# One weight prepared per pair of half steps, transfers issued in pairs, and two small results in one accumulator bank

## The chip, the cores and the metric

The kernel runs on one core of a Trainium2 chip. The metric is the device time of one execution in microseconds (us). The core's engines work at the same time and wait for each other through semaphores: PE (TensorE, matrix products and transposes; its results go to eight accumulator banks in PSUM), DVE (VectorE), ACT (ScalarE), POOL (GpSimd) and SP, which here only issues transfers.

## The reference

Three layers follow each other, all in float32. The first is an attention with two parts: a coarse one over keys and values averaged in groups of four, and a local one in which a query sees the seven keys around it. The second is a mixture of eight experts, whose weights per token come from eight rounds of row and column normalising. The third is a gated product `(x w_a * x w_b) w_out`.

```python
q_d = q.reshape(B, H, Sd, 4, D).mean(axis=3)        # k_d, v_d alike; B, H, S, D = 2, 8, 576, 64
out_up = np.repeat(sm_attn(q_d, k_d, v_d), 4, axis=2)
mask = np.abs(pos[:, None] - pos[None, :]) < 4
out_local = np.matmul(softmax(np.where(mask, scores, -1e9)), v)
x = out_up + out_local                              # (1152, 512) after a transpose
logits = x @ w_gate                                 # P: exp, then 8 times rows and columns normalised
for e in range(8):
    out += P[:, e:e+1] * (np.maximum(x @ w1[e], 0) @ w2[e])
return (out @ w_a) * (out @ w_b) @ w_out
```

## The kernel before, in words

Every float32 factor is kept as a high and a low part (`xh`, `xl`; a weight block's `hi`, `lo`), and each product takes three matmuls. A weight block is made from a raw tile: ACT casts it (line 138), and DVE or POOL subtracts (line 139). All of this is `split`. Raw tiles are two halves of 256 KB times two; two of them can be staged at once, and a new one is fetched when an old one has been used up.

Attention has 24 items, each a pair of heads times a third of a sequence. They run in a software pipeline, the generator `side()`: in step s, item s is transposed and scored, and items s-1 to s-4 are in later stages. A step has two halves, separated by `yield`. The main program runs the first layer of the first two weight units (half of expert 0 each) meanwhile, and calls `side_step()` for a half step at a time. The order of all instructions on each engine is fixed when the program is built.

The stages that matter here, with the lines of the profile:

- `a1` (lines 991, 1005) transposes an item's queries and, where a new pair of heads begins, its keys, which takes a second bank. `a2` and `a4` copy and scale them on ACT; DVE sums the keys in fours (line 1049).
- `b1` and `b1c` score (line 61); `b2` takes maxima on DVE; `b3` exponentiates on ACT (lines 1100 and 1103); `b4` normalises: `pdn` on DVE (line 1120), `p` on POOL (line 1117).
- `c1` transposes the coarse weights `pdn` (line 1130, two instructions into `pt2`) and the local weights `p` (line 1135, three instructions into `pt`); `c2` copies the coarse ones (line 1141, DVE or ACT), `c3` the local ones on ACT (line 1149).
- `d1` multiplies both with v (line 61) into one bank `ps`: columns 0 to 191 local, 192 to 239 coarse. `d2a` scales the coarse part on ACT (`od`, line 1170), `d2` adds both on DVE (`x`, line 1176), and `d3` splits the sum into `xh` (ACT, line 1186) and `xl` (POOL, line 1187).

In the second half of step s the order of the calls is `d1(s-3)`, `d2a(s-3)`, `b3(s-1)`, `c1(s-2)`, `d2(s-3)`, `c2(s-2)`. Items 0 to 10 are scored (`b1`, `b1c`) in the first half of the step after their own; from item 11 on in the second half of their own step, and there `b1c(s)`, four matmuls with `kd`, stands between `d1` and `c1` (steps 11 to 23). So `c1` of item i (1 to 23) always follows `d1` of item i-1 in the same half step.

All attention results use tiles named `at` from a ring of six banks (`psa`). A tile that is asked for gets the bank of the tile six requests ago and waits until that is read. A step takes a bank in `a1` (two with keys), one in `b1`, two in `c1`, one in `d1`.

Around it, `step()` prepares weight blocks by the numbers in `share`, one number for each call, and advances attention by three half steps in two calls. `load_some()` issues one transfer of a raw tile per half step, from a list `coming`.

Of the kernel before, what the change touches and what calls it, by code (L numbers as in the profile page):

```python
# [8 lines left out]
F32 = mybir.dt.float32  # L9
# [11 lines left out]
def attn_moe_glu_kernel(  # L21
# [16 lines left out]
    nc = tc.nc  # L38
# [21 lines left out]
    def mm(o, l, r, start, stop, check=True):  # L60
        nc.tensor.matmul(out=o, lhsT=l, rhs=r, start=start, stop=stop, skip_group_check=not check)  # L61
# [34 lines left out]
    def dve(us, after=None):  # L96
        M.dve = max(M.dve, M.pe if after is None else after) + us

    def act(us):
        M.act = max(M.act, M.pe) + us  # L100
# [20 lines left out]
    def new_block(uses):  # L121
        i = nring[0] % NSLOT
        assert RING[i] is None or RING[i].uses == 0
        nring[0] += 1
        t = wr.tile([128, 1024], F32R, tag=f"w{i}", name=f"w{i}")
        RING[i] = Block(t[:, 0:512], t[:, 512:1024], uses)
        return RING[i]

    def pool(us):
        M.pool = max(M.pool, M.pe) + us  # L130
# [3 lines left out]
    def split(b, raw, k=1, low=None):  # L134
        hi, lo = b.hi, b.lo
        if k > 1:
            hi, lo = (t.rearrange("p (k f) -> p k f", k=k) for t in (hi, lo))
        nc.scalar.copy(out=hi, in_=raw)  # L138
        lows.append(lambda: (low or nc.vector).tensor_tensor(  # L139
            out=lo, in0=raw, in1=hi.bitcast(F32), op=ALU.subtract  # L140
        ))
        if not put_off[0]:
            lows.pop()()
        act(0.6)
        if low is None:
            dve(0.75, 0.0)
        else:
            pool(1.35)
# [10 lines left out]
    wq = []  # L159
# [57 lines left out]
    hold, nsteps, freed, coming = [True], [0], [0], []  # L217

    def fetch():
        while lq and staged[0] < 2:  # L220
            r = lq.pop(0)
            staged[0] += 1
            r.place = stg.tile([128, 2, 512], F32, tag="raw", name="raw", bufs=2)
            r.dmas = r.load(r.place)
            coming.append(r)
            r.at = M.pe
            if not hold[0]:
                r.tile

    def load_some():  # L230

        if nsteps[0] >= max(6, freed[0] + 2):
            fetch()
        while coming and not coming[0].dmas:
            coming.pop(0)
        if coming and nsteps[0] not in NO_LOAD:
            coming[0].dmas.pop(0)()

    def halves(load, left):

        rs = [Raw(lambda t, j=j: load(t, j), left[j]) for j in range(len(left))]
        lq.extend(rs)
        return rs

    def queue_plain(u, uses=6, low=None):

        u.w = {}
        rs = halves(u.load1, (2, 2))
        for i in range(2):
            for j in range(2):  # L250
                def piece(i=i, j=j):
                    b = u.w[i, j] = new_block(uses)
                    split(b, rs[j].tile[:, :, 256 * i:256 * i + 256], 2, low)
                    rs[j].used()
                wq.append(Task(piece, 0.0 if low else 0.68, 1.35 if low else 0.0, ready=rs[j].ready, slot=True))

    def queue_combined(u, low=None):

# [71 lines left out]
    for i, w in enumerate((w_a, w_b, w_out)):  # L330
        t = dram.tile(list(w.shape), F32, name=f"w32_{i}")
        w32.append(t)
        src = w.bitcast(I32).rearrange("a b -> (a b)").rearrange("(c p f) -> c p f", p=128, f=2 * CH)
# [64 lines left out]
    def loader(src):  # L398
        return lambda t, j: [
            lambda k=k: nc.sync.dma_start(out=t[:, k], in_=src[:, 2 * j + k]) for k in range(2)  # L400
        ]

    def half_loader(src):
# [11 lines left out]

        return load

    units = []
    for e in range(E):
        for hf in range(2):  # L420
            u = Unit()
            u.e, u.hf = e, hf
            load = loader if units else half_loader
            u.load1 = load(w1[e][:, hf * 512:(hf + 1) * 512].rearrange("(k p) f -> p k f", p=128))
            u.load2 = loader(w2[e][hf * 512:(hf + 1) * 512, :].rearrange("(k p) f -> p k f", p=128))
            units.append(u)
# [3 lines left out]
    for g in range(GU):  # L430
        u = Unit()
# [447 lines left out]
    ready = [-1]  # L879
    attn_stack = ExitStack()  # L880
    ap_ = attn_stack.enter_context(tc.tile_pool(name="ap", bufs=1, side="right"))
    at = attn_stack.enter_context(tc.tile_pool(name="at", bufs=3, side="right"))
    psa = attn_stack.enter_context(tc.tile_pool(name="psa", bufs=6, space=PSUM))
# [97 lines left out]
        )  # L981
        v_d[b, hp] = vd

    pA, pB, pC, pD = {}, {}, {}, {}

    def a1(i, b, u, hp):

# [136 lines left out]

    def c1(i, b, u, hp):
        p, pd = pB.pop(i)
        pt = psa.tile([128, 512], F32, tag="at", name="at")
        pt2 = psa.tile([128, 512], F32, tag="at", name="at")
        for kh in range(2):
            nc.tensor.transpose(  # L1130
                pt2[0:72, kh * 128:kh * 128 + R],
                pd.rearrange("p (t k) -> p k t", k=2)[:, kh], ident[:R, :R],
            )
        for c in range(NC):
            nc.tensor.transpose(pt[0:W, c * 128:(c + 1) * 128], p[:, c], ident)  # L1135
        pC[i] = pt, pt2
# [15 lines left out]
    def d1(i, b, u, hp):  # L1152
        a, d = pC.pop(i)
        hs = slice(2 * hp, 2 * hp + 2)
        ps = psa.tile([128, 512], F32, tag="at", name="at")
        n = NC * 16
        pd_ = ps[:, UT:UT + n]
        for kh in range(2):
            for h in range(2):
                mm(pd_[64 * h:64 * h + 64], v_d[b, hp][:, kh, h], d[:, kh, h], kh == 0, kh == 1)  # L1160
        for c in range(NC):
            for h in range(2):
                ph = slice(64 * h, 64 * h + 64)
                mm(ps[ph, c * 64:(c + 1) * 64], v_win[b, u, hp][:, c, h], a[:, c, ph], True, True)
        pD[i] = ps, pd_
# [92 lines left out]
    order = [(0, u, hp) for hp in range(HP) for u in range(2)]  # L1258
# [9 lines left out]
    def side():  # L1268
# [17 lines left out]
        for s in range(n + 5):  # L1286
# [34 lines left out]
            if s >= TURN:  # L1321
                do(b1, s)
            do(d1, s - 3)
            if s >= TURN:
                do(b1c, s)
            do(d2a, s - 3)
            do(b3, s - 1)
            do(c1, s - 2)
            do(d2, s - 3)
            do(c2, s - 2)  # L1330
# [8 lines left out]
    TURN = 11  # L1339
# [33 lines left out]
    with tc.manual_schedule():  # L1373
# [19 lines left out]
        for h in range(2):  # L1393
            ph = slice(64 * h, 64 * h + 64)
            for base, cm, st_ in ((9, 1, -1), (-3, -1, 1)):
                nc.gpsimd.affine_select(
                    out=mw[ph], in_=mw[ph], compare_op=ALU.is_ge, fill=-1e30, base=base,
# [8 lines left out]


        for u, low in zip(units[:2], (nc.gpsimd, None)):
            queue_plain(u, low=low)
        for u in units[:2]:  # L1410
            queue_out(u)
        queue_combined(units[2], nc.gpsimd)
# [58 lines left out]
        def side_step():  # L1471
            if not closed:
                nsteps[0] += 1
                load_some()
            if gens[0] is None:
                return
            try:
                next(gens[0])
            except StopIteration:
                if closed:  # L1480
                    gens[0] = None
                else:
                    close_attention()
# [3 lines left out]
        tmp_stack = ExitStack()  # L1487
        turn = 0.0
        nside = 0
        share = [0, 0, 1, 1, 1, 1, 2, 2, 1, 2, 1]  # L1490

        def step():
            nonlocal turn
# [71 lines left out]
        for x, names in (("gh0", ("t1", "b12")), ("gl0", ("b22", "b21"))):  # L1565
            t = gp.tile([128, 1536], F32, tag=x, name=f"t{x}")
# [4 lines left out]
        for x, G in (("h", GH), ("l", GL)):  # L1571
            t = [g0p.tile([128, 1024], F32R, tag=f"g{x}_0{n}", name=f"g{x}_0{n}") for n in range(2)]
# [29 lines left out]
        for x, G in (("h", GH), ("l", GL)):  # L1602
            o = 16 if x == "l" else 0
            t = [gp.tile([128, 1296], F32R, tag=f"g{x}{n}", name=f"g{x}_1{n}") for n in range(2)]
# [93 lines left out]
```

## Time and profile before

| | us |
|---|---|
| median of 3 runs (lowest 1048.74) | 1049.03 |
| profiled execution, whole | 1048.58 |
| span from its first to its last instruction | 1046.8 |
| PE busy | 1037.9 (99%) |
| DVE, ACT, POOL busy | 656.1, 481.1, 528.3 |

Attention, with work of expert 0 beside it, fills about the first 140 us. The rest of the span is experts and the gated product, which the diff does not touch. In the rows, times start at the first instruction; "idle before" is the time in which the engine had nothing before the instruction, with what ended it. PE's ends are modelled, its starts are recorded.

### The profile page before, as it was taken

How to read it: one execution, taken by the hardware profiler on the slowest of the kernel's cores; microseconds unless marked ns; L12 is line 12 of the kernel's file. 1: busy time of each engine (PE TensorE's matmuls, PEld its weight loads, DVE VectorE, ACT ScalarE, POOL GpSimd, SP SyncE). 2: the span in 40 equal slices, each digit the busy share in tenths (PEclk: the TensorE clock that was granted, in tenths of full speed). 3: DMA queues.
4: the chain of work that ended last, by engine and by line, in shares of the span. 5: the costliest groups of instructions: out<-in, count | busy, mean ns of one | idle time of the engine just before them, and what ended most of it. 6: DMA issues, size and time to landing. Idle time of an engine off the chain costs nothing.

```text
span 1046.8 us, 18525 instructions
## 1 busy us (share of the span) xinstructions
PE 1037.9 (99%) x6940; PEld 937.7 (90%) x6940; DVE 656.1 (63%) x1328; ACT 481.1 (46%) x1173; POOL 528.3 (50%) x531
## 2 busy tenths in 40 slices
PE   8999999999999999999999999999999999999998
PEld 6888889899899998999899899989999899999997
DVE  7785548666566565656656565656444685767664
ACT  6764424555444444445444454544343744332320
POOL 5633136647464555647364564746444544655521
PEclk9999999999999999999999999999999999999999
DMA  9662001243323323242433323232110101221102
GB/s 194 149 165 62 10 1 41 71 132 94 117 80 115 102 71 106 66 129 83 112 104 88 106 67 113 95 113 82 61 61 21 41 21 61 61 61 41 34 8 90
DMA packets 80728, 84.53 MB, mean 81 GB/s; under 512 B 35328, under 2 KB 54784, under 8 KB 80640
## 3 DMA queue, kind: packets, MB, share of 16 engines
q1 hardware_dynamic: 78864, 82.92, 27.4%
q8 instruction: 54, 0.88, 0.3%
q10 hardware_dynamic: 1776, 0.44, 0.2%
q14 instruction: 34, 0.28, 0.1%
HBM read 71.54 MB, written 11.80 MB: 80 GB/s over the span
## 4 chain that ended last, share of the span: by engine, by line
PE 95%; DVE 2%; POOL 1%; ACT 1%; issue 1%; DMA 0%; DVEq 0%; ACTq 0%; POOLq 0%
PE g L61 90%; PE at L61 3%; PE at L1130 1%; PE at L1135 1%; PE g L855 0%; PE at L991 0%; POOL w L139 0%; PE at L1005 0%; DVE G L696 0%; ACT p L1100 0%; DMA raw<-w 0%; POOL gl L692 0%; DVE kd L1049 0%; DVE b L621 0%; DVE rsum L1112 0%
## 5 line engine op out<-in xcount | busy, mean ns | idle before, releaser
L61 PE MATMUL g<-w,gh 128*128 128x512 f32 x1314 | 408.0, 392 | 0.0
L61 PE MATMUL g<-xh,w 128*128 128x256 f32 (+2 forms) x1472 | 316.0, 300 | 0.0
L692 POOL TENSOR_TENSOR gl<-G,gh 128x256 fp32r<-128x256 f32 (+1 forms) x216 | 177.8, 832 | 250.1 <-ACT gh L690 244.0
L61 PEld LDWEIGHTS g<-w,gh 128*128 128x128 f32 x1314 | 239.6, 188 | 43.6
L61 PE MATMUL g<-w,gl 128*128 128x512 f32 x657 | 257.6, 392 | 0.0
L61 PEld LDWEIGHTS g<-xh,w 128*128 128x128 f32 x1472 | 242.8, 188 | 2.4
L61 PE MATMUL g<-xl,w 128*128 128x256 f32 (+2 forms) x736 | 220.0, 299 | 0.0
L696 DVE TENSOR_TENSOR G<-g,G 128x256 f32<-128x256 f32 (+1 forms) x400 | 168.3, 451 | 68.6 <-PE g L61 34.5
L61 PE MATMUL g<-Th,w 128*128 128x256 f32 (+1 forms) x960 | 207.5, 294 | 0.4 <-DVE G L696 0.3
L139 DVE TENSOR_TENSOR w<-raw,w 128x512 fp32r<-128x512 f32 x129 | 116.2, 910 | 79.4 <-ACT w L138 79.3
L61 PEld LDWEIGHTS g<-Th,w 128*128 128x128 f32 x960 | 159.7, 188 | 3.3 <-issue 1.0
L548 DVE SCALAR_TENSOR_TENSOR acc<-g,P,acc 128x512 f32<-128x512 f32 x126 | 94.2, 748 | 94.9 <-PE g L61 91.6
L61 PEld LDWEIGHTS g<-w,gl 128*128 128x128 f32 x657 | 123.4, 188 | 26.3
L61 PE MATMUL g<-Tl,w 128*128 128x256 f32 (+1 forms) x480 | 140.7, 293 | 0.0
L61 PEld LDWEIGHTS g<-xl,w 128*128 128x128 f32 x736 | 138.2, 188 | 2.6 <-issue 0.2
L690 ACT CAST gh<-G 128x256 fp32r<-128x256 f32 (+1 forms) x216 | 93.6, 433 | 100.7 <-DVE G L706 85.7
L138 ACT CAST w<-raw 128x512 fp32r<-128x512 f32 x181 | 109.6, 620 | 63.4 <-POOL raw L269 48.3
L688 ACT ACTIVATE G<-G 128x256 f32<-128x256 f32 (+1 forms) x168 | 74.2, 442 | 103.1 <-DVE G L696 103.1
L139 POOL TENSOR_TENSOR w<-raw,w 128x512 fp32r<-128x512 f32 x52 | 68.5, 1324 | 57.7 <-ACT w L138 57.7
L61 PEld LDWEIGHTS g<-Tl,w 128*128 128x128 f32 x480 | 90.3, 188 | 2.1
L381 POOL TENSOR_TENSOR dec<-dec 128x384 int32<-128x384 int32 x48 | 49.4, 1029 | 77.7 <-ACT dec L357 52.3
L139 POOL TENSOR_TENSOR w<-s,w 128x512 fp32r<-128x512 f32 x40 | 55.6, 1391 | 21.1 <-ACT w L138 21.0
(179 smaller groups left out, 990.9 us busy)
## 6 DMA issues: line engine op xcount, KB each, us to landing
raw<-in_moe_w_dram SPq DMA_DIRECT2D x128, 256.0 KB
w<-dec SPq DMA_DIRECT2D x48, 192.0 KB
dec<-in_moe_w_a_dram SPq DMA_DIRECT2D x16, 384.0 KB
dec<-in_moe_w_b_dram SPq DMA_DIRECT2D x16, 384.0 KB
dec<-in_moe_w_out_dram SPq DMA_DIRECT2D x16, 384.0 KB
raw<-w SPq DMA_DIRECT2D x48, 128.0 KB
raw<-w SPq DMA_DIRECT2D x12, 256.0 KB
out_dram<-acc SPq DMA_DIRECT2D x9, 256.0 KB
```

The source lines that it names most:

```text
L61: nc.tensor.matmul(out=o, lhsT=l, rhs=r, start=start, stop=stop, skip_group_check=not check)
L138: nc.scalar.copy(out=hi, in_=raw)
L139: lows.append(lambda: (low or nc.vector).tensor_tensor(out=lo, in0=raw, in1=hi.bitcast(F32), op=ALU.subtract))
L381: nc.gpsimd.tensor_tensor(out=t, in0=t, in1=raw[:, :, 0], op=ALU.add)
L548: nc.vector.scalar_tensor_tensor(out=a, in0=ps, scalar=P[:, tt, u.e:u.e + 1], in1=a, op0=ALU.mult, op1=ALU.add)
L688: nc.scalar.activation(out=src, in_=src, func=AF.Relu)
L690: nc.scalar.copy(out=h, in_=src)
L692: nc.gpsimd.tensor_tensor(out=l, in0=src, in1=h.bitcast(F32), op=ALU.subtract)
L696: nc.vector.tensor_tensor(out=o, in0=bank_, in1=b, op=ALU.add)
L1130: nc.tensor.transpose(pt2[0:72, kh * 128:kh * 128 + R], pd.rearrange("p (t k) -> p k t", k=2)[:, kh], ident[:R, :R],)
L1135: nc.tensor.transpose(pt[0:W, c * 128:(c + 1) * 128], p[:, c], ident)
```

## The change

The diff has four parts.

1. **Shared bank.** `d1` of item i leaves its bank in `shared`, and `c1` of item i+1 puts the two coarse transposes in columns 256 to 511 of that bank rather than in a bank of its own.
2. **Column halves.** The second unit's first-layer weights are loaded in halves by columns (all four row blocks, 256 columns) rather than by rows. `queue_plain` then uses up the first half after two blocks, not three.
3. **Transfers in pairs.** After half step 23, `load_some` issues both transfers of a raw tile together.
4. **Shares.** `share` becomes 0, 0, 1, 1, 3, 1, 1, 1, 2, 1, 1.

```diff
         if coming and nsteps[0] not in NO_LOAD:
-            coming[0].dmas.pop(0)()
+            for _ in range(2 if nsteps[0] > 2 * TURN + 1 else 1):
+                if coming[0].dmas:
+                    coming[0].dmas.pop(0)()
...
-    def queue_plain(u, uses=6, low=None):
+    def queue_plain(u, uses=6, low=None, columns=False):
...
-                    split(b, rs[j].tile[:, :, 256 * i:256 * i + 256], 2, low)
-                    rs[j].used()
-                wq.append(Task(piece, 0.0 if low else 0.68, 1.35 if low else 0.0, ready=rs[j].ready, slot=True))
+                    if columns:
+                        r = rs[i]
+                        raw = r.tile[:, j].rearrange("p (k f) -> p k f", k=2)
+                    else:
+                        r = rs[j]
+                        raw = r.tile[:, :, 256 * i:256 * i + 256]
+                    split(b, raw, 2, low)
+                    r.used()
+                r = rs[i if columns else j]
+                wq.append(Task(piece, 0.0 if low else 0.68, 1.35 if low else 0.0, ready=r.ready, slot=True))
...
+    def column_loader(src):
+        def load(t, i):
+            d = t.rearrange("p a (b c) -> p (a b) c", b=2)
+            return [
+                lambda k=k: nc.sync.dma_start(
+                    out=d[:, 2 * k:2 * k + 2], in_=src[:, 2 * k:2 * k + 2, 256 * i:256 * i + 256]
+                ) for k in range(2)
+            ]
+
+        return load
...
-            load = loader if units else half_loader
+            load = (half_loader, column_loader)[len(units)] if len(units) < 2 else loader
...
     def c1(i, b, u, hp):
         p, pd = pB.pop(i)
+        pt2 = shared.pop(i, None)
+        if pt2 is None:
+            pt2 = psa.tile([128, 512], F32, tag="at", name="at")
+        pt2 = pt2[:, 256:512]
         pt = psa.tile([128, 512], F32, tag="at", name="at")
-        pt2 = psa.tile([128, 512], F32, tag="at", name="at")
...
         ps = psa.tile([128, 512], F32, tag="at", name="at")
+        if i + 1 < len(order):
+            shared[i + 1] = ps
...
-            queue_plain(u, low=low)
+            queue_plain(u, low=low, columns=u is units[1])
...
-        share = [0, 0, 1, 1, 1, 1, 2, 2, 1, 2, 1]
+        share = [0, 0, 1, 1, 3, 1, 1, 1, 2, 1, 1]
```

PE and POOL keep their instructions in the same order; what PE waits for moves. This is PE in the second half of step 12 before (`at` with its number is the bank's tile: 1143 is `d1`'s, 1163 is `pt2`, 1162 is `pt`):

```order
L61 MATMUL at_1143<-pdT_1069,vd1_397 64x48 x3
L61 MATMUL at_1143<-plT_1092,vw_782 64x64 [waits DMAHW6_49]
L61 MATMUL at_1143<-plT_1092,vw_782 64x64
L61 MATMUL at_1134<-kd1_1112,qT0_112 64x144 [waits DVE_49,Activation_49]
L61 MATMUL at_1134<-kd1_1112,qT0_112 48x144
L1130 MATMUL at_1163<-ident_76,pdn_1100 72x112 [waits PE_49]
L1130 MATMUL at_1163<-ident_76,pdn_1100 72x112
L1135 MATMUL at_1162<-ident_76,p0_114 70x128 [waits PE_49,Pool_49]
```

The same place in the changed kernel, where lines 1130 and 1135 have become 1153 and 1158:

```order
L61 MATMUL at_1134<-pdT_1060,vd1_396 64x48 x3
L61 MATMUL at_1134<-plT_1083,vw_776 64x64 [waits DMAHW6_49]
L61 MATMUL at_1134<-plT_1083,vw_776 64x64
L61 MATMUL at_1125<-kd1_1103,qT0_112 64x144 [waits DVE_49,Activation_49]
L61 MATMUL at_1125<-kd1_1103,qT0_112 48x144
L1153 MATMUL at_1134<-ident_76,pdn_1091 72x112 [waits Activation_49]
L1153 MATMUL at_1134<-ident_76,pdn_1091 72x112
L1158 MATMUL at_1153<-ident_76,p0_114 70x128 [waits PE_49,Pool_49]
```

The first coarse transpose now writes `at_1134`, the bank into which `d1` has just put its products, and waits for ACT: the semaphore's value is reached by the `od` of that same bank. It is so in all 23 items from 1 on. On DVE, `x` (`at_1134,od_1147`), which waited for ACT alone, now waits for PE's second coarse transpose as well.

On ACT the casts change places against `od`, the copy of the coarse products. This is ACT in step 13 before, between the relu's output `gh` and `od`:

```order
L1186 CAST xh_79<-x_1169 128x192
L500 ACTIVATE gh1_97<-g1_1206 128x384
L138 CAST w6_1221<-raw_817 128x512
L500 ACTIVATE gh1_97<-g1_1224 128x384
L138 CAST w7_1239<-raw_909 128x512
L1170 ACTIVATE od_1264<-at_1251 128x48
```

And there in the changed kernel:

```order
L1211 CAST xh_79<-x_1159 128x192
L520 ACTIVATE gh1_97<-g1_1199 128x384
L138 CAST w6_1214<-raw_902 128x512
L138 CAST w7_1217<-raw_902 128x512
L138 CAST w8_1220<-raw_1166 128x512
L520 ACTIVATE gh1_97<-g1_1223 128x384
L138 CAST w9_1238<-raw_1166 128x512
L1195 ACTIVATE od_1263<-at_1250 128x48
```

Two more casts stand here, ahead of the second relu; in each of the two steps that follow, one cast stands ahead of `od` rather than two.

## Rows read from the trace of the kernel before

**Rows 1.** The page's parts 1 and 2: PE's busy time, PE's granted clock.

```profile
PE 1037.9 (99%) x6940; PEld 937.7 (90%) x6940; DVE 656.1 (63%) x1328; ACT 481.1 (46%) x1173; POOL 528.3 (50%) x531
...
PEclk9999999999999999999999999999999999999999
```

**Rows 2.** The page's part 4: the chain of waits, by engine.

```profile
PE 95%; DVE 2%; POOL 1%; ACT 1%; issue 1%; DMA 0%; DVEq 0%; ACTq 0%; POOLq 0%
```

**Rows 3.** Busy us by stretch: PE, PEld, DVE, ACT, POOL; granted clock, DMA share, GB/s.

```profile
0.00:10.00 10.00, 8.17 (x76) 5.75 (x76) 4.87 (x33) 4.58 (x13) 2.22 (x14) 1.00 0.84 164
...
20.00:30.00 10.00, 9.86 (x153) 8.28 (x154) 8.19 (x30) 8.53 (x34) 8.90 (x13) 1.00 0.94 194
...
60.00:70.00 10.00, 9.09 (x115) 7.87 (x111) 8.63 (x23) 8.64 (x29) 3.66 (x5) 1.00 0.76 208
```

**Rows 4.** What PE waited for in 0 to 200: us, times, longest.

```profile
PE at L1005 <- ACT pd L1103: 0.9, 1, 0.9
PE at L1130 <- DVE pdn L1120: 0.6, 2, 0.4
```

**Rows 5.** Timeline of PE, steps 11 and 23: start, us, instructions.

```profile
44.15 0.53 PE L61 MATMUL at<-plT,vw 70*64 70x64 f32 x12
44.52 0.41 PE L61 MATMUL at<-kd,qT 128*64 128x144 f32 x4
44.86 0.41 PE L1130 MATMUL at<-ident,pdn 112*72 112x112 f32 x2
...
116.15 0.42 PE L1130 MATMUL at<-ident,pdn 112*72 112x112 f32 x2
```

**Rows 6.** Timeline of ACT at the same two places.

```profile
44.79 0.21 ACT L1170 ACTIVATE od<-at 128x48 f32<-128x48 f32 x1 [0.52 <-PE at L61]
...
116.08 0.21 ACT L1170 ACTIVATE od<-at 128x48 f32<-128x48 f32 x1 [0.74 <-PE at L61]
```

**Rows 7.** Timeline of PE: coarse transposes of items 4, 6 and 8.

```profile
23.03 0.42 PE L1130 MATMUL at<-ident,pdn 112*72 112x112 f32 x2
...
29.41 0.42 PE L1130 MATMUL at<-ident,pdn 112*72 112x112 f32 x2
...
35.74 0.42 PE L1130 MATMUL at<-ident,pdn 112*72 112x112 f32 x2
```

**Rows 8.** Timeline of ACT in the same half steps.

```profile
23.89 0.32 ACT L1060 ACTIVATE kd<-kd 128x144 f32<-128x144 f32 x1 [0.35 <-DVE kd L1049]
24.12 0.19 ACT L1170 ACTIVATE od<-at 128x48 f32<-128x48 f32 x1
...
29.59 0.21 ACT L1170 ACTIVATE od<-at 128x48 f32<-128x48 f32 x1 [0.26 <-PE at L61]
...
36.79 0.21 ACT L1170 ACTIVATE od<-at 128x48 f32<-128x48 f32 x1
```

**Rows 9.** Timeline of PE in step 14: item 12's coarse transposes, item 15's keys.

```profile
61.07 0.42 PE L1130 MATMUL at<-ident,pdn 112*72 112x112 f32 x2
...
61.82 0.41 PE L1005 MATMUL at<-ident,kn 96*128 96x96 f32 x3
63.15 0.47 PE L1005 MATMUL at<-ident,kn 96*128 96x96 f32 x3 [0.91 <-ACT pd L1103]
```

**Rows 10.** Timeline of ACT there.

```profile
61.47 0.62 ACT L138 CAST w<-raw 128x512 fp32r<-128x512 f32 x1 [0.49 <-DMA raw<-in_moe_w_dram]
61.99 0.20 ACT L1170 ACTIVATE od<-at 128x48 f32<-128x48 f32 x1
...
62.70 0.40 ACT L1103 ACTIVATE pd<-at,nd 112x144 f32<-112x144 f32 x1
```

**Rows 11.** Timeline of DVE in step 11.

```profile
45.03 0.36 DVE L1176 TENSOR_TENSOR x<-at,od 128x192 f32<-128x192 f32 x1
45.66 0.38 DVE L1112 TENSOR_REDUCE rsum<-p 128x3 f32<-128x213 f32 x1 [0.27 <-ACT p L1100]
```

**Rows 12.** Engines idle before they used a raw tile, by what ended it.

```profile
  DMA raw<-in_moe_w_dram: 2.9, 4
```

More of the change, by code (lines that the diff above doesn't have):

```diff
@@ L982, in sum_vd @@
         v_d[b, hp] = vd
-    pA, pB, pC, pD = {}, {}, {}, {}
+    pA, pB, pC, pD, shared = {}, {}, {}, {}, {}
     def a1(i, b, u, hp):
```

## Prediction

> **What bounds the kernel now.** I read the page from the top. PE is busy 1037.9 us of a span of 1046.8 [rows 1], and the chain of waits runs through PE for 95% of it [rows 2]. So a change counts where PE stands idle, or is made to. The diff alters only attention, so I next took the stretches of the first 140 us: PE has idle time at the start (8.17 of 10 us busy), while everything fills up, and 0.91 us between 60 and 70; from 20 to 30 PE is at 9.86, with DVE, ACT and POOL all above 8 [rows 3]. What PE waited for there is little: 0.9 us once, for an exponential on ACT, and 0.6 us in two waits for `pdn` [rows 4]. All that the change can win on PE by shorter waits is thus about 1 us; the rest of the reading asks what it makes PE wait for anew.
>
> **The ring of banks, the gain.** The 0.91 us is a wait of the ring: the second three key transposes of item 15 need the bank from which `pd` is still read; `pd` ended at 62.70 + 0.40 = 63.10, PE went on at 63.15 [rows 9, 10]. This also gives what a wait on ACT costs beyond ACT's own end: 0.05 us. With a bank fewer per step the ring reaches a step's share further back, and the order shows PE's own instructions as what is waited for there. `pd` was late because two casts stood ahead of it on ACT, the second of them idle 0.49 us for its transfer [rows 10]; the new shares leave one. Both causes go: **-0.91 us**.
>
> **The shared bank, the cost.** Item i's coarse transposes write the bank that `d1` of item i-1 has just filled, and from which ACT still has to read `od`. So on PE there is now a round trip inside a half step: last product, `od` on ACT, first coarse transpose. Before, `od` ran beside the transposes. I price it as the time at which `od` ended, plus 0.05, less the time at which the transposes started.
>
> - *Steps 11 to 23 (items 9 to 21).* Between the products and the transposes lie four matmuls with `kd`, 0.34 us from 44.52 to 44.86 [rows 5]. ACT starts `od` at 44.79, and what ended its idle time was PE, so it cannot start sooner. It ends at 45.00; PE may go on at 45.05 instead of 44.86: 0.19 us [rows 5, 6]. The last one gives the same: 116.08 + 0.21 + 0.05 against 116.15, 0.19 [rows 5, 6]. Items 12 and 13 had ACT later, for the casts that are moved away: item 12 would otherwise cost 61.99 + 0.20 + 0.05 against 61.07, 1.17 us [rows 9, 10]. I count both at 0.19. 13 x 0.19 = **+2.5 us**.
> - *Steps 24 and 25 (items 22 and 23)* have no `kd` matmuls as cover. The nearest row without cover is item 6: `od` 29.59 to 29.80, PE at 29.41, so 0.44 us [rows 7, 8]. 2 x 0.44 = **+0.9 us**.
> - *Steps 3 to 10 (items 1 to 8)* have no cover either, and in the three steps that transpose keys (items 2, 4 and 8) ACT comes late by itself: it copies the keys, waits for DVE's sums, scales them (`kd` at 23.89), and only then reaches `od`. Item 4: 24.12 + 0.19 + 0.05 against 23.03, 1.33 us. Item 8: 36.79 + 0.21 + 0.05 against 35.74, 1.31 us [rows 7, 8]. The upper bound takes every item at its own lateness: 3 x 1.33 + 5 x 0.44 = 6.2. The lower bound supposes that ACT sets the pace alone (8.53 of 10 busy [rows 3]) and is not moved, so that only the last lateness stays: 1.31. I walk between: 1.33 at item 4, which takes in items 1 to 3; 3 x 0.44 for items 5 to 7, less 0.2 because PE arrives late and finds `pdn` ready; 0.9 of the 1.31 at item 8, since ACT has followed PE by then in part only. **+3.3 us**. Nothing gives it back: from 37 us on PE has no idle time to close.
>
> **DVE behind it.** `x` must now wait for PE's second coarse transpose, so it goes from 45.03 to about 45.05 + 0.41 + 0.05 = 45.5. Queued behind it is `rsum`, which itself waited 0.27 us for ACT and started at 45.66 [rows 11]; with 0.36 us for `x` it starts about 0.2 us later. Its result reaches PE one step on, 4 us later. I count nothing; without that cover it is 0.2 x 13 = 2.6 us, which I keep for the upper end.
>
> **Transfers, halves, shares.** The same bytes are loaded and the same blocks made. Issuing in pairs puts a transfer ahead of the loads of queries and keys on SP's queue, but these are for two steps later. The idle time before a use of raw tiles, for want of a transfer from the weights, was 2.9 us in 4 waits over the whole run [rows 12]; one of them, 0.49, is counted above. The order puts four casts instead of two ahead of `od` in step 13. ACT has idle time of its own before `od` (0.52 and 0.74 us [rows 6]) and waits for PE before the relu, so casts whose tiles have landed cost nothing. If the third has not landed, the wait of [rows 10] comes back there: +0.5 to +1.2 us, upper end.
>
> **A rule against the change.** Rows: before, `od` (44.79 to 45.00) and the transposes (from 44.86) ran at once, in different banks [rows 5, 6]; after, their columns are still disjoint, 192 to 239 against 256 to 511. The Trainium skill, page "PSUM — Partial Sum Buffer", section "PSUM bank collisions raise a hardware error", has PSUM guarded by bank and quadrant of partitions, not by address, so that disjoint columns do not help. By addresses alone the sum would be -0.9; by that rule the round trip has to be paid, and the order's new wait agrees. No run here shows a collision.
>
> **Sum.** -0.91 + 2.5 + 0.9 + 3.3 = +5.8 us on the profiled execution's 1048.58: 1054.4. The median of the runs lies 0.45 above that execution, so **1054.8 us**. By the bounds (early 1.31 to 6.2, DVE 0 to 2.6, casts 0 to 1.2): +3.8 to +12.5, of which the upper end needs everything to go wrong at once; I take +3 to +9 as this case's own range.
>
> **Rivals.**
>
> - *The round trip is hidden, or the change does not bring it:* ACT reads `od` sooner, or PE's waits elsewhere shrink by as much. For it: PE and ACT already wait on each other in every step, and what PE loses at `c1` it may save at `p` and `pdn`. Against it: ACT's `od` was held by PE in rows 6, and PE had only about 1 us of waits to save [rows 4]. Time: 1049.03 - 0.9 = 1048.1. It is the rival on the faster side. 13%.
> - *ACT's queue becomes the pace.* A cast that waits for its transfer now holds up PE directly through `od`. Price: 1.17 us [rows 9, 10] for every such step. With four of them, +5.8 + 4.7 = 1059.5. It decides when ACT's wait for transfers grows beyond the 2.9 us of [rows 12]. 11%. Slower by 2% would need thirteen such steps of the 23; at most 1% of its chance.
> - *PE's clock falls.* The granted clock is full in all forty slices, also in the first 10 us, with PE idle for 18% [rows 1, 3]. The new idle time in steps 3 to 10 is about 3.3 us in 25, or 13%, less than that. If the clock fell to 1.2 GHz from step 3 to 10, PE's work there, some 22 of 24 us, would take up to twice as long: +22 us, 1077. It decides if a stretch between 13 and 37 us shows a granted clock below 1.00. 4%. The Trainium skill, page "TensorE: Matmul & The Clock Gate", section "HAM oscillation — how this bites in real kernels", warns of idle gaps that bring the clock down; the trace shows gaps without it.
>
> **Chances and range.** Forecast 72%, hidden 13%, ACT 11%, clock 4%. A measurement of this kernel can tell about 2%, 21 us, from no change; only the clock case and a remnant of the others reach that, on the slow side: faster 1%, same 95%, slower 4%. The range is from 1048.0, which takes in the hidden case, to 1058.5, the forecast's upper end; the clock, most of the ACT case and the forecast's tails, some 18%, lie outside. The forecast's own range is 1052 to 1058.
>
> **What the profile after would show.** Right: among PE's waits the line of the coarse transposes behind ACT's `od`, some 23 times and about 6 us in all; about 0.15 us of idle time each in steps 11 to 23 and over 1 us at items 4 and 8; no wait of the key transposes for `pd`; the end of attention some 5 to 6 us later and everything after it unchanged. Wrong: those waits absent, or present with the end of attention not moved, which would mean that PE made them good elsewhere in steps 3 to 10; or ACT idle for a raw tile in step 13.

## The result, and the profile after

The changed kernel takes **1055.89 us**, median of 6 runs (1054.96 to 1056.63), against 1048.88 us for the kernel before, median of 6 on the same chip. The medians differ by 7.0 us; the ratio is 1.0068, 95% interval [1.0055, 1.0082], which is 5.8 to 8.6 us. One execution of the kernel before took 1402.92 us, against 1047.98 to 1049.41 for its other five, and the ratio leaves it out. The change is slower by more than the remaining runs of either kernel differ among themselves, but by less than 2%. The prediction was 1054.8, of 1048.0 to 1058.5.

The profiled execution took 1056.63 us, with a span of 1054.8. The page after: busy time, PE's granted clock, the chain of waits [rows 1, 2].

```profile
PE 1040.4 (99%) x6940; PEld 938.8 (89%) x6940; DVE 656.4 (62%) x1328; ACT 484.3 (46%) x1173; POOL 528.5 (50%) x531
...
PEclk9999999999999999999999999999999999999999
...
PE 96%; DVE 2%; ACT 1%; issue 1%; DMA 0%; POOL 0%; ACTq 0%; DVEq 0%
...
PE g L61 90%; PE at L61 3%; PE at L1153 1%; PE at L1158 1%; ACT od L1195 0%; PE g L875 0%; PE at L1011 0%; PE at L1025 0%; DVE kd L1069 0%; ACT w L138 0%; DMA raw<-w 0%; ACT p L1120 0%; DVE nm L1110 0%; DVE b L641 0%; DVE G L716 0%
```

The page of the profile hardly differs. The same 6940 matmuls are there, and 40 slices of 26 us are too coarse for what happened; only the last row has something new, `od` (now L1195) and the coarse transposes (now L1153) as links of the chain. The first row of what PE waited for in the first 200 us says it outright: us, times, longest [rows 4].

```profile
PE at L1153 <- ACT od L1195: 5.9, 10, 1.2
```

No row for `pd` is left, and a new one of 5.9 us stands at the top. It counts ten times, not 23: in the 13 late items the four matmuls with `kd` run up to the wait, and what is left is too short to be listed. The stretches show both kinds; the columns are those of [rows 3].

```profile
20.00:30.00 10.00, 8.17 (x137) 6.95 (x135) 7.56 (x27) 7.63 (x29) 8.34 (x11) 1.00 0.84 189
...
40.00:50.00 10.00, 10.00 (x90) 9.04 (x90) 4.30 (x13) 4.33 (x12) 2.19 (x5) 0.83 0.67 170
60.00:70.00 10.00, 9.74 (x127) 8.71 (x126) 9.20 (x24) 8.87 (x28) 4.05 (x5) 1.00 0.88 219
...
38.00:40.00 2.00, 0.76 (x20) 0.62 (x17) 1.57 (x4) 1.51 (x6) 1.22 (x2) 0.98 0.93 258
40.00:42.00 2.00, 2.00 (x10) 1.72 (x8) 1.55 (x6) 1.33 (x5) 1.34 (x3) 0.50 0.64 139
```

From 20 to 30 PE has fallen from 9.86 of 10 us busy to 8.17. From 60 to 70 it has risen from 9.09 to 9.74: the wait for `pd` is gone, the short waits are left (0.13 us at item 9, from the `kd` products' end at 50.14 + 0.41 to 50.68). And one thing is new: after 38 to 40, with PE busy for 0.76 of 2 us, the granted clock is 0.50 from 40 to 42, that is 1.2 GHz, and 0.83 on average over 40 to 50.

Now the round trips themselves. PE's timeline: the coarse transposes of items 4, 6 and 8 [rows 7]; then step 11 with the `kd` products ahead [rows 5]; then item 15's key transposes, now L1025 [rows 9].

```profile
24.93 0.42 PE L1153 MATMUL at<-ident,pdn 112*72 112x112 f32 x2 [1.08 <-ACT od L1195]
...
31.66 0.42 PE L1153 MATMUL at<-ident,pdn 112*72 112x112 f32 x2 [0.37 <-ACT od L1195]
...
39.75 0.52 PE L1153 MATMUL at<-ident,pdn 112*72 112x112 f32 x2 [1.24 <-ACT od L1195]
...
50.14 0.41 PE L61 MATMUL at<-kd,qT 128*64 128x144 f32 x4
50.68 0.42 PE L1153 MATMUL at<-ident,pdn 112*72 112x112 f32 x2
...
68.29 0.66 PE L1025 MATMUL at<-ident,kn 96*128 96x96 f32 x6
```

And ACT's timeline in the same half steps [rows 6, 8], with the casts of step 13 last:

```profile
24.45 0.32 ACT L1080 ACTIVATE kd<-kd 128x144 f32<-128x144 f32 x1 [0.35 <-DVE kd L1069]
24.68 0.19 ACT L1195 ACTIVATE od<-at 128x48 f32<-128x48 f32 x1
...
31.40 0.21 ACT L1195 ACTIVATE od<-at 128x48 f32<-128x48 f32 x1 [0.47 <-PE at L61]
...
39.49 0.21 ACT L1195 ACTIVATE od<-at 128x48 f32<-128x48 f32 x1
...
50.42 0.21 ACT L1195 ACTIVATE od<-at 128x48 f32<-128x48 f32 x1 [0.52 <-PE at L61]
...
59.24 1.65 ACT L138 CAST w<-raw 128x512 fp32r<-128x512 f32 x3
```

In each place `od`'s end plus 0.05 to 0.06 us is the transposes' start: 24.68 + 0.19 to 24.93, 31.40 + 0.21 to 31.66, 39.49 + 0.21 to 39.75, 50.42 + 0.21 to 50.68. The three casts of step 13 run back to back and wait for no transfer. The six key transposes of item 15 run in one piece.

**Where the time went**, from the starts of the coarse transposes in both traces (the gate's products after attention end 8.1 us later, the span is 8.0 longer):

| from item to item | before, us | after, us | more | predicted |
|---|---|---|---|---|
| start to 0 | 10.29 | 10.36 | 0.07 | 0 |
| 0 to 8 | 25.45 | 29.39 | 3.94 | 3.3 |
| 8 to 9 | 9.12 | 10.93 | 1.81 | 0.19 |
| 9 to 23 | 81.02 | 83.34 | 2.32 | 2.25 |

The 1.6 us too many from 8 to 9 are the stretch at half clock. They belong to this execution, the slowest of the six: its mean granted clock is 0.998, that of the five others (1054.96 to 1056.36 us) 0.999 or 1.000. Such an execution is not the change's alone: one of 17 of the kernel before, timed beside experiments 5 to 8, took 1051.93 us at 0.997. Without the 1.6 us the items take some 6.5 us more than before.

### The profile page after: what moved, and what is told of

It reads as the page before. It is cut to its first block, busy times and chain, and to the rows that moved or that the text cites. A ratio compares the mean times of both kernels' runs of the same rounds, so it can differ in the third digit from the quotient of the medians.

```text
span 1054.8 us, 18535 instructions
## 1 busy us (share of the span) xinstructions
PE 1040.4 (99%) x6940; PEld 938.8 (89%) x6940; DVE 656.4 (62%) x1328; ACT 484.3 (46%) x1173; POOL 528.5 (50%) x531
## 4 chain that ended last, share of the span: by engine, by line
PE 96%; DVE 2%; ACT 1%; issue 1%; DMA 0%; POOL 0%; ACTq 0%; DVEq 0%
PE g L61 90%; PE at L61 3%; PE at L1153 1%; PE at L1158 1%; ACT od L1195 0%; PE g L875 0%; PE at L1011 0%; PE at L1025 0%; DVE kd L1069 0%; ACT w L138 0%; DMA raw<-w 0%; ACT p L1120 0%; DVE nm L1110 0%; DVE b L641 0%; DVE G L716 0%
```

## Experiments

All were timed against the kernel before on the same chip. Own theory: the round trip through the shared bank is the whole loss, its price is what `od` ends later than the independent work on PE, and the casts' new places win back 0.9. Rivals: ACT's queue and its transfers, the clock, DVE's later `x`.

**1. Own banks: the change without its shared bank**

```diff
-        if i + 1 < len(order):
-            shared[i + 1] = ps
```

> The changed kernel with part 1 alone undone: the coarse transposes have a bank of their own again; column halves, paired transfers and the new shares stay. Theory (the round trip over ACT is the whole cost, and the 0.91 us wait of item 15's key transposes goes because one cast fewer stands ahead of pd, not because of the ring): about 0.9 us under the kernel before, 1048.0, PE's line of coarse transposes waiting for od empty, clock 1.00 everywhere. Rival A (the other three parts cost part of the 7 us): 1050 or more, with ACT idle for raw tiles. Rival B (the looser ring is what took the 0.91 us away): as the kernel before, 1048.9, with the key transposes' wait for pd back.

Measured: 1048.68 us, ratio 0.9999 [0.9990, 1.0008]. PE has no wait for `od` left. In step 14, PE first, then ACT:

```profile
62.40 0.42 PE L1153 MATMUL at<-ident,pdn 112*72 112x112 f32 x2
...
63.15 0.81 PE L1025 MATMUL at<-ident,kn 96*128 96x96 f32 x6
```

```profile
61.70 0.61 ACT L138 CAST w<-raw 128x512 fp32r<-128x512 f32 x1
62.33 0.21 ACT L1193 ACTIVATE od<-at 128x48 f32<-128x48 f32 x1
...
63.04 0.40 ACT L1123 ACTIVATE pd<-at,nd 112x144 f32<-112x144 f32 x1
```

One cast ahead of `od` instead of two, and the key transposes run in one piece (0.81 us for the six where 0.66 is usual, so that at most 0.15 of the wait is left), although the ring is as tight as before: item 12 to 13 takes 5.02 us instead of 6.00. So the shared bank is the whole loss, and the other three parts take the wait for `pd` away by themselves. The expectation named 1048.0. That the time itself shows no gain had to be asked further (2).

**2. Own banks, profiled twice more** (the same kernel)

> The same kernel as in the run with own banks, for a second profiled execution. Question: why the 0.9 us between items 12 and 13, which its trace shows, is not in its time. Theory: the first 10 us come in two speeds whatever the kernel, worth 1.1 us, and the execution profiled first had the slower; an execution whose first coarse transposes start at 10.3 takes 1047.8 +- 0.2, one in which they start at 11.4 takes 1048.9 +- 0.2. Rival (something late in attention gives the 0.9 back): 1048.5 or more with a start at 10.3.

> The same once more, for a third profiled execution: 1047.8 +- 0.2 with the first coarse transposes at 10.3, 1048.9 +- 0.2 with them at 11.4; the rival gives 1048.5 or more in either case.

Measured: 1047.94 and 1048.19 us, one execution each. The first coarse transposes start at 10.50 and 10.64; in the execution of (1), which took 1048.98, they started at 11.44. Time less start: 1037.44, 1037.55, 1037.54; for the kernel before 1048.58 - 10.29 = 1038.29. That is the theory, not the rival: from the first item on, three executions agree within 0.11 us and are 0.74 to 0.85 shorter than the profiled one of before, and the rest of the spread among the three is the start. (The third time lies 0.19 above the band that was given for a start at 10.3; it started 0.34 later, after PE had waited 0.45 us for a transfer of keys.) Here is one row of PE's timeline in the first 10 us, as it stands in the execution of (1), then in the one of 1047.94, and last, for comparison, the same kind of row in the profile of the changed kernel, from the stretch at half clock:

```profile
6.82 0.90 PE L61 MATMUL at<-kT,qT 64*64 64x70 f32 x12
```

```profile
6.68 0.53 PE L61 MATMUL at<-kT,qT 64*64 64x70 f32 x12
```

```profile
42.30 0.90 PE L61 MATMUL at<-kT,qT 128*64 128x70 f32 x12
```

The same twelve matmuls take 0.90 us in one and 0.53 in the other; PE gets to its full pace later. And 0.90 is what twelve such matmuls took where the clock was granted at 0.50 (from 42 to 43 us), so the slow start looks like a longer time at 1.2 GHz, although its row of the granted clock says 1.00. Of the 13 profiled executions of all kernels here three have these matmuls at 0.90 or 0.91 and start the first coarse transposes at 11.43 to 11.79; the ten others have 0.53 and start at 10.11 to 10.64. Still, medians over all runs don't separate the kernels (interval of (1)). The 0.8 is shown in the traces, not in the times; whether each execution of the kernel before has its wait of 0.91 us is open, as only one was profiled.

**3. The shared bank alone**, put into the kernel before

```diff
+        pt2 = shared.pop(i, None)
+        if pt2 is None:
+            pt2 = psa.tile([128, 512], F32, tag="at", name="at")
+        pt2 = pt2[:, 256:512]
...
-        pt2 = psa.tile([128, 512], F32, tag="at", name="at")
...
+        if i + 1 < len(order):
+            shared[i + 1] = ps
```

> The kernel before with part 1 alone: the shared bank, old transfers and shares. Theory: before plus 4.0 (items 1 to 8) plus 1.1 to 1.7 (lower clock around 40 us) plus 2.5 plus 0.9 (items 9 to 23), plus about 1.4 since in steps 14 and 15 two casts again stand ahead of od, less 0.9 for the ring: 1058, with waits of about 1.2 and 0.6 us at items 12 and 13. Rival A: clearly under the changed kernel, 1053 or less. Rival B: no wait of key transposes for pd in either.

Measured: 1055.86 us, ratio 1.0073 [1.0059, 1.0086], the same as the whole change. PE's largest wait, then ACT and PE in step 14:

```profile
PE at L1133 <- ACT od L1175: 6.6, 11, 1.2
```

```profile
64.89 1.13 ACT L138 CAST w<-raw 128x512 fp32r<-128x512 f32 x2
65.92 0.21 ACT L1175 ACTIVATE od<-at 128x48 f32<-128x48 f32 x1
...
66.63 0.41 ACT L1103 ACTIVATE pd<-at,nd 112x144 f32<-112x144 f32 x1
```

```profile
66.18 0.42 PE L1133 MATMUL at<-ident,pdn 112*72 112x112 f32 x2 [0.52 <-ACT od L1175]
...
66.93 0.66 PE L1005 MATMUL at<-ident,kn 96*128 96x96 f32 x6
```

With the old shares two casts hold up `od`, and through it PE. The key transposes don't wait. But this does not show the looser ring at work: held up behind `od`, they start at 66.93, the second three are due some 0.22 us later (half of the 0.44 us to the next matmul at 67.37), and `pd` has ended by then, at 66.63 + 0.41 = 67.04. The expectation was 2 us high: in this kernel's profile the clock did not fall, and items 12 and 13 cost it 0.84 us more than the changed kernel rather than 1.4.

**4. Shared late and shared early: the bank shared for items 9 to 23 only, and for items 1 to 8 only**

```diff
-        if i + 1 < len(order):
+        if 9 <= i + 1 < len(order):
```

```diff
-        if i + 1 < len(order):
+        if i + 1 < 9:
```

> The changed kernel with the bank shared only from item 9 on (where four kd matmuls, or none in the last two steps, stand between). Theory: the terms of steps 11 to 25 alone, before minus 0.9 plus 2.5 plus 0.9: 1051.4, clock 1.00 throughout since PE is not idle in steps 3 to 10. Rival (the late handshakes are covered by the kd matmuls after all and the early ones are everything): 1048.

> The changed kernel with the bank shared only up to item 8. Theory: before minus 0.9 plus 4.0 plus 1.1 to 1.7 for the clock: 1053.2, with the granted clock below 1.00 somewhere between 38 and 46 us in the profile or in some of the runs. Rival (the fall of the clock needs nothing of the early waits): clock 1.00 here and lower in the kernel that shares late only.

Measured: late 1052.09 us, ratio 1.0036 [1.0024, 1.0049]; early 1051.80, 1.0034 [1.0022, 1.0047]. The losses, 3.6 and 3.3 us, add up to 6.9; the whole change has 7.0. That is closer than it should be, since each of the two kernels has the gain of 0.91 us and the sum counts it twice; the late kernel's profiled execution, which is also its median, has the slow start of (2), with the first coarse transposes at 11.43. The traces are the cleaner reading: items 8 to 23 take 2.45 us more in the late kernel, and items 0 to 8 take 3.92 more in the early one, the whole change's 3.94. The early kernel's expectation, 1053.2, had 1.1 to 1.7 us for the clock in it; its clock did not fall in the profile. The early kernel's stretches around item 8:

```profile
38.00:40.00 2.00, 0.76 (x21) 0.62 (x21) 1.71 (x4) 1.51 (x7) 1.05 (x2) 1.00 0.95 273
40.00:42.00 2.00, 2.00 (x28) 1.74 (x28) 1.50 (x6) 1.92 (x8) 1.45 (x3) 1.00 0.64 140
```

PE is as idle as in the changed kernel's profile, 0.76 of 2 us busy, and the clock stays. So the fall there needs more than that idle time, and the 3.9 us are without it.

**5. Local transposes first: independent work put into the round trip**

```diff
+        for c in range(NC):
+            nc.tensor.transpose(pt[0:W, c * 128:(c + 1) * 128], p[:, c], ident)
...
-        for c in range(NC):
-            nc.tensor.transpose(pt[0:W, c * 128:(c + 1) * 128], p[:, c], ident)
```

The loop over the local transposes moves ahead of the coarse ones, within `c1`.

> The changed kernel with the two kinds of transposes in c1 exchanged: the three local ones, which go to a bank of their own, come first and lie between the last product and the first coarse one. Theory (what is paid is the uncovered part of the round trip): about 0.25 to 0.33 us more cover. Steps 11 to 23 wait no longer (13 x 0.2 = 2.6 less), items 22, 23, 1, 3, 5, 6 and 7 about 0.3 less each (2.1), items 2, 4 and 8 the same 0.3 less (0.9), if the local weights p, which POOL makes last, are there in time: 1055.9 - 5.6 = 1050.3. Rival (it is a fixed price of a wait on ACT, cover or not): 1055.9.

Measured: 1050.21 us, ratio 1.0013 [1.0005, 1.0022]. PE's waits, then PE in the next step with keys' products:

```profile
PE at L1155 <- ACT od L1195: 2.2, 3, 0.8
...
PE at L1153 <- POOL p L1137: 0.8, 2, 0.5
```

```profile
53.12 0.41 PE L61 MATMUL at<-kd,qT 128*64 128x144 f32 x4
53.47 0.52 PE L1153 MATMUL at<-ident,p 128*70 128x128 f32 x3
53.82 0.36 PE L1155 MATMUL at<-ident,pdn 112*72 112x112 f32 x2
```

Three transposes, 0.35 us from 53.47 to 53.82, cover the 0.19 us that were left open, and PE is busy for all of 40 to 70 us. Only the items with keys, where `od` is late by over a microsecond, still wait. The expectation was 1050.3. 5.7 of the 7.0 us come back from an exchange of two loops.

**6. `od` first: in the first steps, `od` put ahead of the copies of the next queries and keys**

```diff
-            if s < TURN:
-                do(a4, s)
             if s >= TURN:
                 do(b1, s)
             do(d1, s - 3)
             if s >= TURN:
                 do(b1c, s)
             do(d2a, s - 3)
+            if s < TURN:
+                do(a4, s)
```

> The changed kernel with ACT's scaling of the key sums (kd) put behind od in steps up to 10, where it stood ahead of it. Theory (in the three key steps PE waits for ACT's queue, in which kd waits for DVE): the waits of items 2, 4 and 8 fall from 1.08 to 1.24 to the 0.37 of the others, 2.3 us less: 1053.5. Rival (the late od comes from PE's own products or from ACT's copies of the keys): no change, 1055.9.

Measured: 1053.44 us, ratio 1.0043 [1.0031, 1.0055]. PE's waits, and ACT at item 4:

```profile
PE at L1153 <- ACT od L1195: 3.6, 9, 0.6
```

```profile
23.61 0.25 ACT L1195 ACTIVATE od<-at 128x48 f32<-128x48 f32 x1
24.11 0.33 ACT L1080 ACTIVATE kd<-kd 128x144 f32<-128x144 f32 x1 [0.24 <-DVE kd L1069]
```

As expected (1053.5). The longest wait halves, from 1.2 to 0.6 us, when `od` does not stand behind `kd` and its wait for DVE. Items 2, 4 and 8 now wait 0.37, 0.61 and 0.49 us; what stays is, for the most part, the bare round trip.

**7. After x: `c1` called behind `d2`, so that both readers of the bank stand in the way**

```diff
-            do(c1, s - 2)
             do(d2, s - 3)
+            do(c1, s - 2)
```

> The changed kernel with the call of d2 ahead of c1, so that the coarse transposes wait for DVE's x, which waits for od: the round trip made longer by one DVE instruction. Theory: 0.36 us for x plus 0.05 per wait, 23 times, 0.39 to 0.46 each: 1055.9 + 9.7 = 1065.6. Rival (PE is not held by the round trip in most steps): less than 3 us more.

Measured: 1073.02 us, ratio 1.0236 [1.0215, 1.0258], slower and 7.4 us above what was expected. PE's largest wait, and the stretches:

```profile
PE at L1153 <- DVE x L1201: 19.1, 23, 1.6
```

```profile
10.00:20.00 10.00, 6.74 (x105) 5.37 (x104) 7.45 (x25) 6.54 (x26) 6.10 (x8) 1.00 0.98 194
20.00:30.00 10.00, 8.36 (x93) 6.81 (x91) 5.32 (x18) 5.34 (x20) 5.39 (x7) 0.51 0.61 149
30.00:40.00 10.00, 8.13 (x101) 6.81 (x102) 5.13 (x19) 5.67 (x22) 5.64 (x9) 0.81 0.33 76
```

PE's waits for the second reader, 19.1 us, are near the 17.2 us that the expectation adds to the kernel before. What was not foreseen is the clock: it was granted at 0.51, about the 1.2 GHz level, from 20 to 30 us, after a stretch with PE busy for 6.74 of 10 us. At the granted clock the two stretches lost at most 10 x 0.49 + 10 x 0.19 = 6.8 us of PE's pace, which is about the miss. It was so in every execution of this kernel: their mean granted clocks are 0.985 to 0.994.

**8. The shares alone**, put into the kernel before

```diff
-        share = [0, 0, 1, 1, 1, 1, 2, 2, 1, 2, 1]
+        share = [0, 0, 1, 1, 3, 1, 1, 1, 2, 1, 1]
```

> The kernel before with the new list of shares alone: old banks, row halves, single transfers. Theory (the 0.91 us wait at item 15's keys came from the second cast ahead of pd and its missing transfer): the wait is gone here too, 1048.0, unless the third cast of step 13 finds its tile not landed; then ACT is idle for a transfer there, up to 1 us late. Rival (the paired transfers and column halves are needed): the wait stays, or ACT is idle for a raw tile in step 13 and PE behind it: 1048.5 or more.

Measured: 1051.90 us, 3.5 above the kernel before, ratio 1.0031 [1.0020, 1.0042]: the rival, and more than the 1 us that the theory allowed for a late tile. ACT, then PE, in step 13 and 14, then the stretch behind them:

```profile
57.33 0.62 ACT L138 CAST w<-raw 128x512 fp32r<-128x512 f32 x1 [2.82 <-DMA raw<-in_moe_w_dram]
...
59.46 0.40 ACT L1103 ACTIVATE pd<-at,nd 112x144 f32<-112x144 f32 x1
```

```profile
59.92 0.47 PE L1005 MATMUL at<-ident,kn 96*128 96x96 f32 x3 [2.37 <-ACT pd L1103]
```

```profile
60.00:70.00 10.00, 10.00 (x114) 9.11 (x116) 8.04 (x23) 7.02 (x23) 4.22 (x6) 0.83 0.65 150
```

With halves by rows and single transfers the third cast waits 2.82 us for its tile, and everything on ACT behind it is late, `pd` and the key transposes too. That is only half of the loss: from item 9 to 23 this trace is 3.02 us longer than before, of which the wait that grew from 0.91 to 2.37 is 1.46. After it the clock falls, to 0.83 on average from 60 to 70, at most 1.7 us; five of the six executions have a mean granted clock of 0.996 or 0.998, and the one at 1.000 is the fastest, 1051.37. In (1), which has the same shares with both other parts, no cast there waits. So column halves and paired transfers are what makes the shares possible; which of the two does more was not tried.

**9. Filler: the wait filled with matmuls that nobody needs**

```diff
+        for _ in range({2: 8, 4: 8, 8: 8}.get(i, 2) if 1 <= i <= 8 else 0):
+            mm(pt[:, :256], wz[:, 0:128], wz, True, True)
```

> The changed kernel with added matmuls on zeros, before the coarse transposes of items 1 to 8, into the bank of the local transposes (which are written over them): eight for items 2, 4 and 8, two for each other item. They stand where PE waits for od. Theory (PE waits for the reader, the clock is no matter): the added work lies inside the wait, so the time stays that of the changed kernel's undisturbed clock, 1055.4 +- 0.7; PE's idle time behind od falls from 5.9 us to under 3 us, and the coarse transposes of item 8 start at 39.7 +- 0.5 as before; the clock is 1.00 in every stretch from 20 to 60. Rival (the loss is the clock's, which the idle gaps bring down): with the gaps filled the time falls towards 1052.

Measured: 1055.08 us, ratio 1.0060 [1.0043, 1.0077]. A stretch, then PE at item 8:

```profile
38.00:40.00 2.00, 1.74 (x30) 1.32 (x27) 1.64 (x4) 1.50 (x7) 1.15 (x2) 1.00 0.66 193
```

```profile
38.52 1.05 PE L61 MATMUL at<-wz 128*128 128x256 bf16 x8
39.83 0.42 PE L1155 MATMUL at<-ident,pdn 112*72 112x112 f32 x2 [0.26 <-ACT od L1197]
```

PE now looks busy, 1.74 of 2 us, its waits for `od` fall from 5.9 to 1.9 us, and the coarse transposes of item 8 start at 39.83 instead of 39.75, in both traces 29.39 us behind item 0's. The clock is 1.00 throughout, and the time stays. The idle time was room, not a cause: it is the round trip that costs, and the clock has no part in the loss but for the 1.6 us of the one profiled execution. One thing in this trace was not foreseen: at item 12 a cast ahead of `od` waits 0.74 us for its raw tile, and PE 0.86 us for `od`. So with the changed kernel's transfers too, a tile can come late and hold up PE through the shared bank; in the changed kernel's own profile no cast of steps 13 to 15 waits for one.

## Why the prediction was right

It was right in its mechanism and nearly in its size: +5.8 foreseen, +7.0 measured. Of the 1.1 us by which the median lies above the 1054.8, some 0.6 is the term of items 1 to 8; the rest is not located, as only one execution was profiled. Its end of attention came 8.1 us later where 5 to 6 were foreseen, 1.6 of it by the clock. By its steps:

- **The ring, -0.91.** The wait is gone. "Both causes go" said too much: with the ring untouched (1) it goes too, so in the change the casts' new places are enough. What the looser ring would do by itself is not shown: in (3) the transposes come too late to need it. The gain shows in the traces; in the times of (1) it is inside the interval.
- **Steps 11 to 25, 13 x 0.19 + 2 x 0.44.** Single steps confirm it: item 9 to 10 went from 4.87 to 5.07 us, +0.20; the last two items from 5.57 and 4.16 to 6.09 and 4.60, +0.52 and +0.44. From item 9 to 23, with the gain, 2.32 against 2.25 foreseen.
- **Items 1 to 8, +3.3.** The mis-sized term: 3.94, and 3.92 in the early kernel of (4). By the walk's own parts: 1.33 at item 4 was to take in items 1 to 3, but 1.83 was lost by then (12.74 us from item 0 before, 14.57 after). Item 2 had cost 1.35 already, only 0.47 of it was made good at item 3, and item 4 cost 0.95 more. Items 5 to 7 took 0.79 instead of 1.1. Item 8 took 1.32 instead of 0.9: its lateness came in full, with a wait of 1.24 us.
- **DVE, nothing.** Right: the 2.32 us from item 9 to 23 leave no room for the 2.6 kept for it. In step 11 `x` ran later against the transposes, and `rsum` did not: 0.80 us behind them both times (44.86 to 45.66 [rows 5, 11], 50.68 to 51.48):

```profile
51.20 0.36 DVE L1201 TENSOR_TENSOR x<-at,od 128x192 f32<-128x192 f32 x1 [0.47 <-PE at L1153]
51.48 0.36 DVE L1132 TENSOR_REDUCE rsum<-p 128x3 f32<-128x213 f32 x1
```

- **Transfers, halves, shares, nothing.** Right for the whole change, as no cast in step 13 waits. But the cover was not named well: it is the other two parts of the change, and without them the shares cost 3.5 us (8), more than the upper end of 1.2 that was given for it. That end had no term for the clock, which is about half of it.
- **The rule on banks.** Waiting for `od` is what the program's order asks for. No run let the transposes write beside the read, so whether the chip would bear that stays untried. What the runs add is the price of obeying: all of the loss.
- **Rivals.** Hidden: refuted. PE made good a part only: at items 1 to 8 it waited 5.2 us for `od` in 8 waits (early kernel of (4)), and 3.92 of them were lost. ACT's queue as the pace: not in this change; a late tile holds PE up through `pd` in (8), and once through `od` in (9), for 0.86 us. The clock: it fell after all, in one execution, for about 3 us behind step 10 and not from step 3 to 10, 1.6 us instead of 22. That the trace of before had gaps at the full clock did not rule it out.

No kernel here beats the one before clearly; own banks (1, 2) are its equal in time, 0.8 us shorter in the traces.

## What to carry to other kernels

Sharing a bank between a result that is still to be read and the next write turns a reader beside the critical engine into a round trip on it; its price at each place is the reader's end plus the hop (0.05 us here), less the time at which the writer could have started, and independent work put in between takes off what it covers (5). Look in particular for what stands ahead of the reader on its own queue: a copy of about 0.2 us made PE wait over 1 us in each of the three places where it stood behind another engine's result. And a part of a change that costs nothing may do so only because of another part; cost it alone too.

## What the runs showed of the hardware

- TensorE's granted clock fell after equal idle time in one execution and not in others: with PE busy for 0.76 of 2 us, it was 0.50 in the next 2 us of the changed kernel's profile and 1.00 in the early kernel's (4). With more idle time, 6.74 of 10 us busy, it was 0.51 for 10 us (7); after a single wait of 2.37 us it was 0.83 over 10 us (8). The page "TensorE: Matmul & The Clock Gate" of the Trainium skill, section "HAM oscillation — how this bites in real kernels", warns of idle gaps on TensorE that bring the clock down; these rows agree that they can, and show that they need not.
- The start comes in two speeds: the same twelve matmuls took 0.90 and 0.53 us in two executions of one kernel, and attention began 0.9 us apart (2). The granted clock stands at 1.00 in the rows of both, so that row doesn't tell the two apart. Twelve such matmuls took 0.90 us also where the clock was granted at 0.50, in the changed kernel's profile; that the slow start is the 1.2 GHz level is likely by this, and not shown. Why it lasts longer in some executions was not found.
